# Attention and SwiGLU FFN on one core: the V loads on another DMA queue, and the q parts of the FFN's last products in other places

## The chip, the cores and the metric

The kernel runs on one core of a Trainium2 chip. A core has TensorE (matrix products, PE in the profile; PEld are its weight loads), VectorE (DVE), ScalarE (ACT) and GpSimd (POOL), and SyncE (SP), which computes nothing and issues DMAs. Each engine works off its own queue in program order, and the engines wait for each other by semaphores. A DMA is issued by an instruction in the queue of an engine (SPq and ACTq are the rows of SyncE and ScalarE that do this); the 16 DMA engines of the core then carry it out. The metric is the time of one execution on the device in microseconds, and of several runs the median.

## What is computed

The reference, cut to what matters (B=1, S=2048 rows, D=640; 32 heads of 192; the window W is the last 512 keys; F=1536):

```
xn = layernorm(x)
q = xn @ wq                                  # 32 heads of 192
p = softmax(q @ k[-512:].T * 192**-0.5)      # by head
s = concat(p @ v[-512:]) @ wo
g = silu((silu(xn @ w_gate) * (xn @ w_up)) @ w_down)
out = x + s * g
```

## The kernel before, in words

The order of the instructions in each engine's queue is that of the program text: a manual schedule, in which the framework only adds the waits.

*FFN part (to about 168 us of the profile).* The rows are worked on in four blocks of 512 (b = 0 to 3). For a block, `ffn_hidden` makes twelve groups of columns (f) of silu(gate) * up into the tile hT. The product with w_down is made by `ffn_down(b, u)`, two units a block (u = 0, 1), each with seven products of sums (Strassen's scheme in Winograd's form) in place of eight: w1, w2, w6, w5_, w7, w3, w4, six matmuls of 320 columns each (L456), called in this order, and then `rest`. Three PSUM banks U, V, W of a ring of four take the products; ScalarE copies banks out (L474, L484, L490) and makes the gates (`gate`, L465), VectorE adds (`total`, L462). S1 to S4 are sums of hT columns that are the left sides of w5_, w6, w7 and w3; S1 and S2 are made inside w1. The units of block b - 1 are spread among the column groups of block b; those of the last block have nothing to be spread among. At L678 to L687 they are run one after the other, and among their products the kernel puts six q parts, `q_full(i, j)` for the first two row blocks of head pair 0 (five matmuls of 512 columns into one bank of a score tile, L517, and a copy by ScalarE, L521), and the six sums that are left in the list `xwork` (VectorE, L537). After each product `do()` of number n = 0 to 6, a q part follows for n in (0, 3, 5), and one of `xwork` for each n from 1 on while there is one. The list is empty after the first unit. Behind `rest` of the second unit, ScalarE loads the table for Exp (L688).

*Attention part (to about 705 us).* Heads go in 16 pairs. A pair has four row blocks and two halves; a half is a scores phase (`scores_phase`) and a stretch of contexts (`stretch`). The scores phase has eight `scores` (6 products each into a score tile of PSUM, L777, then Exp by ScalarE into p_t, L781; two such tiles are in rotation), and in slots between them the products that make q of a later half: `differences` (L723), `sides` (L723, copied by ScalarE from PSUM to m_f, L753), `across` (VectorE and GpSimd), `third(0)`, `sums`, `third(1)` (the two `third` are `q_rows`: L709 and a sum by VectorE, L714). `third(0)` writes the PSUM tile that `sides` used, so it waits for the copy L753. The first half of a pair has one group more, `q_diag` (L723, copied by VectorE). The program order on ScalarE at the start of a half is: Exp of the first scores, copy of `sides`, and Exp of the second scores.

The stretch then makes four units of contexts, p times V (L816), in the order of `CONTEXTS`; V_p, one buffer for a head pair, is the right side. At the end of a unit `divide(i, q2)` divides by the row sums (VectorE L834 and L839, ScalarE L845) into O_b, and asks SyncE for a DMA that transposes O_b into OT_b (L848). The last unit of a pair is block 3 with q2 = 1.

`beside(pr, n)` puts side work behind scores n = 0 to 15 of pair pr. At n = 0 it asks for the transpose of the next pair's K on SyncE (`transpose_k`, L192), and then for V of this pair (`load_v(pr)`): two DMAs of 192 KB, one a head, on ScalarE's queue (L182). At n = 10 and 12 it loads wq and K of the pair after the next (SyncE, L148 and L137), and at n = 4, 5, 12, 13 `spill` stores finished OT_b blocks to DRAM (SyncE, L857).

*Last part (to the end).* The product with wo, again seven products for eight (L931), the gate and the store.

Of the kernel before, what the change touches and what calls it, by code (L numbers as in the profile page):

```python
# [10 lines left out]
ALU = mybir.AluOpType  # L11
# [4 lines left out]
def kernel(  # L16
# [13 lines left out]
    nc = tc.nc  # L30
# [14 lines left out]
    NB = Sq // 512  # L45
# [34 lines left out]
    def sc_tile():  # L80
        return sc_pool.tile([P, 2, 512], f32, name="sc")

    def mm_tile(which=None):
        which = mm_next[0] if which is None else which
        mm_next[0] = 1 - which
        return mm_pool[0].tile([P, 2, 512], f32, name="mm", tag="mm%d" % which)
# [92 lines left out]

    def load_v(pr):  # L180
        for h in range(2):
            nc.scalar.dma_start(  # L182
                out=V_p[:, :, h, 0:Dh],
                in_=vv[2 * pr + h, k0:Sk, :].rearrange("(p j) d -> p j d", j=KC),
            )

    def transpose_k(pr):
        d = pairs[pr]
        d["KT"] = kpool.tile([P, KC * 3, P], bf, name="KT")
        d["ssum"] = kpool.tile([P, 3], f32, name="ssum")  # L190
        d["nmean"] = kpool.tile([P, 3], f32, name="nmean")
        nc.sync.dma_start_transpose(  # L192
            out=d["KT"][:, :, :], in_=d["K"][:, :, :, :].rearrange("p j h d -> p (j h d)")
        )
# [4 lines left out]
    def sum_k(pr, c):  # L199
        nc.vector.reduce_sum(pairs[pr]["ssum"][:, c : c + 1], chunk_of_k(pr, c), axis=AX.XY)  # L200
# [3 lines left out]
    def centre_k(pr, n):  # L204

        d = pairs[pr]
        if n == 0:
            d["khat"] = kpool.tile([P, 3, W], bf, name="khat", bufs=2)
            nc.vector.tensor_scalar(d["nmean"][:], d["ssum"][:], -1.0 / W, None, op0=ALU.mult)
        t, dst, c, src = CENTRE[n]  # L210
        nc.vector.tensor_scalar(
            d["khat"][dst, t, :].rearrange("p (j n) -> p j n", n=P), chunk_of_k(pr, c)[src],
            d["nmean"][src, c : c + 1], None, op0=ALU.add,
        )
# [8 lines left out]
    def q_of(i, j):  # L223
        return q_pair(i)[:, 3 * (i % 2) + j, :]
# [4 lines left out]
    with ExitStack() as fctx:  # L229
# [190 lines left out]
        def carve(k, n):  # L420
            part, room[k] = room[k][:, 0:n], room[k][:, n:]
            return part
# [6 lines left out]
        S1, S2, S3, S4 = (carve(k, KD * P).rearrange("p (c q) -> p c q", q=P) for k in (1, 2, 2, 3))  # L429
# [12 lines left out]
        def ffn_down(b, u):  # L442

            if not down_banks:
                down_banks.extend(t[:, n, 0:HC] for t in (mm_tile(), mm_tile()) for n in range(2))
            at = 3 * (2 * b + u)
            U, V, W = (down_banks[(at + k) % 4] for k in range(3))
            g = {}

            def a(side, k):  # L450
                rows = slice((u + 2 * side) * P, (u + 2 * side + 1) * P)
                return hTs[b][:, k * KD : (k + 1) * KD, rows]

            def mm(m, left, ps, first=True):
                for c in range(KD):
                    nc.tensor.matmul(  # L456
                        ps, left[:, c, :], D_OF[m][:, c, :],
                        start=(first and c == 0), stop=(c == KD - 1), skip_group_check=True,
                    )

            def total(to, x, y, op=ALU.add):
                nc.vector.tensor_tensor(to, x, y, op)  # L462

            def gate(side, n, x):
                nc.scalar.activation(g[side][:, n * HC : (n + 1) * HC], x, ACT.Silu)  # L465

            def store(side):
                nc.sync.dma_start(out=g_d[4 * b + u + 2 * side, :, :], in_=g[side][:])

            def w1():  # L470
                for side in range(2):
                    g[side] = ffa.tile([P, D], bf, name="g_t", bufs=2)
                mm(W1, a(0, 0), U)
                nc.scalar.copy(p1, U)  # L474
                total(S1, a(1, 0), a(1, 1))
                total(S2, S1, a(0, 0), ALU.subtract)

            def w2():
                mm(W2, a(0, 1), V)
                total(p1, V, p1)  # L480

            def w6():
                mm(W6, S2, U, False)
                nc.scalar.copy(u2, U)  # L484
                gate(0, 0, p1)
                total(S3, a(0, 0), a(1, 0), ALU.subtract)

            def w5_():
                mm(W5, S1, W)
                nc.scalar.copy(w5, W)  # L490
                total(S4, a(0, 1), S2, ALU.subtract)

            def w7():
                mm(W7, S3, U, False)
                total(w5, U, w5)

            def w3():
                mm(W3, S4, W, False)
                total(u2, W, u2)
                gate(1, 1, w5)  # L500

            def w4():
                mm(W4, a(1, 1), U, False)
                gate(1, 0, U)
                store(1)

            def rest():
                gate(0, 1, u2)
                store(0)

            return [w1, w2, w6, w5_, w7, w3, w4], rest

        def q_full(i, j):
            pr, b = divmod(i, NB)
            q_ps = sc_tile()[:, 0, :]
            for c in range(NC):
                nc.tensor.matmul(  # L517
                    q_ps[:, :], pairs[pr]["wq"][:, AS_IS[j], c, :], xnT[:, c, b * 512 : (b + 1) * 512],
                    start=(c == 0), stop=(c == NC - 1),
                )  # L520
            nc.scalar.copy(q_of(i, j), q_ps[:, :])  # L521
# [81 lines left out]
        xwork = []  # L603
# [74 lines left out]
        early_q = [(i, j) for i in range(2) for j in range(3)]  # L678
        for u in range(2):
            downs, rest = ffn_down(NB - 1, u)  # L680
            for n, do in enumerate(downs):
                do()
                if n in (0, 3, 5):
                    q_full(*early_q.pop(0))
                if xwork and n:
                    xwork.pop(0)()
            rest()  # L687
        nc.scalar.activation(act_t[:], one_t[:], ACT.Exp)  # L688
# [10 lines left out]
    last = NPAIR - 1  # L699
# [130 lines left out]
    def divide(i, q2, acc, by_dve):  # L830
        O_b, OT_b = Obs[i], OTs[i]
        r = smpool.tile([P, 2, 2, 1], f32, name="r")
        a_v = acc[:, :, :].rearrange("p k (h c) -> p k h c", h=2)
        nc.vector.reciprocal(r[:], a_v[:, :, :, Dh : Dh + 1])  # L834
        for k in range(2):
            qt = 2 * q2 + k
            a_k = a_v[:, k, :, :]
            if k in by_dve:
                nc.vector.tensor_tensor(  # L839
                    O_b[:, qt, :, :], a_k[:, :, 0:Dh], r[:, k, :, :].to_broadcast([P, 2, Dh]),  # L840
                    ALU.mult,
                )
                continue
            for h in range(2):
                nc.scalar.activation(  # L845
                    O_b[:, qt, h, :], a_k[:, h, 0:Dh], ACT.Copy, scale=r[:, k, h, :]
                )
        nc.sync.dma_start_transpose(  # L848
            out=OT_b[:, 6 * q2 : 6 * q2 + 6, :],
            in_=O_b[:, 2 * q2 : 2 * q2 + 2, :, :].rearrange("p t h d -> p (t h d)"),  # L850
        )

    def spill(i, eng=nc.sync, qts=slice(0, 4)):

        pr, b = divmod(i, NB)
        at = o_d[4 * b + qts.start : 4 * b + qts.stop, :, 3 * pr : 3 * pr + 3, :]
        eng.dma_start(  # L857
            out=at.rearrange("t p c q -> p t c q"),
            in_=OTs[i][:, 3 * qts.start : 3 * qts.stop, :].rearrange("p (t c) q -> p t c q", c=3),
        )  # L860
# [106 lines left out]
    def total(to, x, y, op=ALU.add):  # L967
        V.tensor_tensor(to, x, y, op)
# [80 lines left out]
    def beside(pr, n):  # L1049

        b, kc = divmod(n, KC)
        if pr < last:
            if n == 0:
                transpose_k(pr + 1)
            elif b == 2 and kc < 3:
                sum_k(pr + 1, kc)
            elif n >= 11:
                centre_k(pr + 1, n - 11)
        if n == 0:
            load_v(pr)  # L1060
        elif pr + 2 < NPAIR and n in (10, 12):
            (load_k if n == 12 else load_wq)(pr + 2)
        half, n8 = divmod(n, 2 * KC)
        prev = pr * NB + 2 * half - 2
        if prev >= 0 and n8 in (4, 5):
            spill(prev + n8 - 4)
        if (pr, n) in AHEAD:
            what, *args = AHEAD[pr, n]
            what(*args)
# [52 lines left out]
    i = last * NB  # L1122
# [70 lines left out]
```

## Time and profile before

| | |
|---|---|
| median of 3 runs | 890.23 us |
| the three runs | 888.45, 890.23, 895.27 us |
| profiled execution, its own time | 893.5 us |
| its span, first to last instruction | 891.7 us |
| mean granted clock of TensorE | 0.998 |
| instructions | 22945 |
| ScalarE's Exp of the scores (L781) | 256, mean 1024 ns, 253.7 us |
| first and last issue of V on ScalarE's queue | 169.6 and 680.9 us |

A row of the timeline reads: start in us, duration in us, engine, line, operation, output tile <- input tiles, shapes, count; in brackets the idle time of the engine just before and what ended it. Neighbouring instructions of one kind are merged into one row, whose duration is that from the first's start to the last's end. Matmuls overlap in the pipeline, so such a row reaches some 0.15 us into the next. A row of the table of waits reads: who waited <- for whom: us in total, times, longest. A row of a table of stretches reads: from:to, length, and then the busy time of PE, PEld, DVE, ACT and POOL in it with the number of instructions, the granted TensorE clock, the share of the DMA engines and GB/s. The chain of waits is the sequence of work and waits, followed back from the end of the run, that set the end.

### The profile page before, as it was taken

The page shows a single profiled execution, that of the slowest core. Times are in us where ns is not written, and L with a number is a line of the kernel's source. Part 1 is how long each engine was busy: PE and PEld are TensorE (multiplying, and loading weights), DVE is VectorE, ACT ScalarE, POOL GpSimd, SP SyncE. Part 2 cuts the span into 40 slices and gives each one's busy share as a digit, 9 for nine tenths or more (in the row PEclk, how much of TensorE's full clock was granted, in tenths as well). Part 3 has the DMA queues.
Part 4 walks back from the last instruction along what each step waited for, and adds up shares of the span by engine and source line. Part 5 has one row for each costly group of instructions (what it writes and reads, how often), then busy time and mean ns, then how long its engine had stood idle before and what let it go on. Part 6 is the DMA issues. An engine that isn't in the chain of part 4 may idle for free.

```text
span 891.7 us, 22945 instructions
## 1 busy us (share of the span) xinstructions
PE 872.3 (98%) x9641; PEld 577.4 (65%) x9657; DVE 603.6 (68%) x1028; ACT 427.7 (48%) x649; POOL 114.0 (13%) x217
## 2 busy tenths in 40 slices
PE   8999999999998999999999999999999999999998
PEld 5455555576675666666666766766756777777775
DVE  5766876676775776767767866866866457555553
ACT  4265433656764765666666666666666400000000
POOL 0000000012212132132132132132120000000000
PEclk9999999999999999999999999999999999999999
DMA  9669873367988979968989777969789998655510
GB/s 295 163 212 279 210 223 97 65 135 155 220 198 172 198 171 202 181 152 194 180 169 199 161 146 176 192 154 207 158 192 264 244 330 311 207 178 177 177 67 16
DMA packets 273432, 165.52 MB, mean 186 GB/s; under 512 B 174384, under 2 KB 268208, under 8 KB 272816
## 3 DMA queue, kind: packets, MB, share of 16 engines
q1 hardware_dynamic: 254928, 149.79, 69.4%
q10 hardware_dynamic: 18400, 14.26, 5.9%
q8 instruction: 76, 1.25, 0.6%
q14 instruction: 28, 0.23, 0.1%
HBM read 89.95 MB, written 40.24 MB: 146 GB/s over the span
## 4 chain that ended last, share of the span: by engine, by line
PE 86%; DMA 6%; ACT 2%; ACTq 2%; DVE 2%; SPq 1%; issue 1%; DVEq 0%
PE acc L931 19%; PE sc L777 15%; PE sc L394 11%; PE mm L723 10%; PE mm L816 9%; PE sc L816 8%; PE mm L709 8%; PE mm L456 5%; DMA OT_b<-O_b 3%; ACTq L182 2%; ACT m_f L753 2%; DMA o_d<-OT_b 1%; PE sc L517 1%; DMA x_t<-in_A_x_dram 1%; DMA OT_b<-O_last 1%
## 5 line engine op out<-in xcount | busy, mean ns | idle before, releaser
L781 ACT ACTIVATE p_t<-sc 128x1024 bf16<-128x1024 f32 x256 | 253.7, 1024 | 61.9 <-PE sc L777 57.3
L777 PE MATMUL sc<-qT,khat 64*128 64x512 bf16 x1536 | 198.7, 377 | 0.0
L816 PEld LDWEIGHTS <-p_t 64*128 64x128 bf16 x4096 | 173.0, 94 | 8.6
L777 PEld LDWEIGHTS <-khat 64*128 64x128 bf16 x1536 | 89.2, 94 | 75.5 <-issue 1.0
L816 PE MATMUL mm<-V_p,p_t 64*128 64x193 bf16 x2112 | 111.6, 243 | 0.0
L816 PE MATMUL sc<-V_p,p_t 64*128 64x193 bf16 x1984 | 104.8, 243 | 0.0
L709 PE MATMUL mm<-xnT,wq_p 64*128 64x512 bf16 x660 | 84.0, 380 | 10.9 <-ACT m_f L753 9.9
L723 PE MATMUL mm<-xc,wq_p 64*128 64x512 f16 x750 | 94.5, 376 | 0.0
L931 PEld LDWEIGHTS <-a_s 128*128 128x128 f16 x768 | 75.1, 98 | 29.2
L714 DVE TENSOR_REDUCE qT<-mm 128x512 bf16<-128x1024 f32 x66 | 80.6, 1223 | 16.1 <-PE mm L709 13.7
L761 POOL TENSOR_TENSOR m_f<-m_f 128x1024 f32<-128x1024 f32 x28 | 65.7, 2348 | 189.2 <-DVE qT L756 189.2
L723 PEld LDWEIGHTS <-wq_p 64*128 64x128 f16 (+1 forms) x1050 | 58.5, 94 | 48.2 <-issue 0.6
L845 ACT ACTIVATE O_b<-sc,r 128x192 bf16<-128x192 f32 x120 | 43.9, 418 | 87.2 <-PE sc L816 87.2
L931 PE MATMUL acc<-b_w,a_q 128*128 128x320 bf16 (+1 forms) x576 | 81.8, 299 | 0.2 <-ACT xc L981 0.2
L931 PE MATMUL acc<-b_w,a_s 128*128 128x320 f16 (+1 forms) x576 | 81.8, 299 | 0.0
L981 ACT COPY xc<-acc 128x320 f32<-128x320 f32 x8 | 3.4, 428 | 141.6 <-PE acc L931 95.7
L931 PEld LDWEIGHTS <-a_q 128*128 128x128 bf16 x576 | 56.3, 98 | 22.4 <-issue 0.6
L709 PEld LDWEIGHTS <-wq_p 64*128 64x128 bf16 x660 | 36.8, 94 | 49.3 <-issue 18.7
L756 DVE TENSOR_TENSOR qT<-mm,m_f 128x1024 bf16<-128x1024 f32 x30 | 36.7, 1225 | 43.7 <-ACT m_f L753 43.7
L394 PE MATMUL sc<-xnT,wu_sb 128*128 128x512 bf16 (+1 forms) x260 | 60.3, 354 | 0.6 <-DMA wu_sb<-in_B_w_up_dram 0.6
L394 PE MATMUL sc<-xnT,wg_sb 128*128 128x512 bf16 (+1 forms) x247 | 59.7, 353 | 1.0
L401 ACT ACTIVATE sg<-sc 128x512 bf16<-128x512 f32 x46 | 27.3, 595 | 68.0 <-PE sc L394 66.2
(110 smaller groups left out, 907.9 us busy)
## 6 DMA issues: line engine op xcount, KB each, us to landing
o_d<-OT_b SPq DMA_DIRECT2D x64, 384.0 KB, 5.5
a_q<-o_d SPq DMA_DIRECT2D x28, 768.0 KB, 5.8
won<-in_A_wo_dram SPq DMA_DIRECT2D x24, 320.0 KB, 4.2
wo_d<-wo_s SPq DMA_DIRECT2D x24, 320.0 KB, 2.9
wq_rows<-in_A_wq_dram SPq DMA_DIRECT2D x16, 480.0 KB, 4.9
wq_rows<-in_A_wq_dram SPq DMA_DIRECT2D x30, 240.0 KB, 6.0
K_p<-in_A_k_cache_dram SPq DMA_DIRECT2D x32, 192.0 KB, 6.2
V_p<-in_A_v_cache_dram ACTq DMA_DIRECT2D x32, 192.0 KB, 4.0
```

Source lines behind the costliest of these rows:

```text
L394: nc.tensor.matmul(out, w_sb[:, c, f * P : (f + 1) * P], xnT[:, c, qc], start=(c == 0), stop=(c == NC - 1),)
L456: nc.tensor.matmul(ps, left[:, c, :], D_OF[m][:, c, :], start=(first and c == 0), stop=(c == KD - 1), skip_group_check=True,)
L709: nc.tensor.matmul(q_ps[:, h, :], w[r, AS_IS[j], c, :], xnT[r, c, b * 512 : (b + 1) * 512], start=(c == 0), stop=(c == NC - 1),)
L714: nc.vector.reduce_sum(q_of(i, j), q_ps[:, :, :].rearrange("p h n -> p n h"), axis=AX.X)
L723: nc.tensor.matmul(ps[:, h, :], ws[h][r, c, :], xs[h][r, c, :], start=(first and c == 0), stop=(c == NC - 1), skip_group_check=True,)
L756: nc.vector.tensor_tensor(q_pair(i)[:, 1:4:2, :], st["ps"][:, :, :], m_f[:, SIDE_S, ::-1, :], ALU.add)
L761: eng.tensor_tensor(m_f[:, SIDE_S, :, :], diag, m_f[:, SIDE_S, :, :], ALU.subtract)
L777: nc.tensor.matmul(sc[:, h, :], khat[r, j, ks], q_of(i, j)[r, :], start=(j == 0), stop=(j == 2))
L781: nc.scalar.activation(p_t[:, :, :], sc[:, :, :], ACT.Exp, scale=scale)
L816: m = nc.tensor.matmul(acc[:, k, h * 256 : h * 256 + Dh + 1], Ps[i][kc][r, h, qt * P : (qt + 1) * P], V_p[r, kc, h, 0 : Dh + 1], start=(p ...
L845: nc.scalar.activation(O_b[:, qt, h, :], a_k[:, h, 0:Dh], ACT.Copy, scale=r[:, k, h, :])
L931: nc.tensor.matmul(ps[k] if ns > 1 else ps, at[:, c, :], b_w[m][:, c, k * w : (k + 1) * w], start=(first and c == 0), stop=(c == KH - 1), ...
```

## The change

Two things, in one diff.

V: `load_v` issues on `nc.sync` in place of `nc.scalar`. V of pair 0 is still asked for behind the first scores of pair 0 (`beside`, n = 0, behind `transpose_k(1)`), now on SyncE. V of each later pair is asked for in `divide` of the last unit of the pair before, behind the division and ahead of the last transpose of that pair; SyncE then waits for the last contexts, which read the one buffer V_p.

FFN: in the two last units the q parts stand otherwise. In the first unit one is put ahead of w1, then one behind each of the products 3 (w5_) and 6 (w4); in the second, behind 1 (w2), 3 and 6. The sums of `xwork` follow products 1, 3 and 5 of each unit. S1 and S2 of the first of these units are asked for when the unit is set up, ahead of its products.

```
     def load_v(pr):
         for h in range(2):
-            nc.scalar.dma_start(
+            nc.sync.dma_start(
...
+            def sums():
+                total(S1, a(1, 0), a(1, 1))
+                total(S2, S1, a(0, 0), ALU.subtract)
+
             def w1():
...
                 mm(W1, a(0, 0), U)
                 nc.scalar.copy(p1, U)
-                total(S1, a(1, 0), a(1, 1))
-                total(S2, S1, a(0, 0), ALU.subtract)
+                if (b, u) != (NB - 1, 0):
+                    sums()
...
+            if (b, u) == (NB - 1, 0):
+                sums()
             return [w1, w2, w6, w5_, w7, w3, w4], rest
...
             downs, rest = ffn_down(NB - 1, u)
+            if u == 0:
+                q_full(*early_q.pop(0))
             for n, do in enumerate(downs):
                 do()
-                if n in (0, 3, 5):
+                if n in ((3, 6), (1, 3, 6))[u]:
                     q_full(*early_q.pop(0))
-                if xwork and n:
+                if xwork and n in (1, 3, 5):
                     xwork.pop(0)()
             rest()
...
+        pr, b = divmod(i, NB)
+        if (b, q2) == (NB - 1, 1) and pr < last:
+            load_v(pr + 1)
         nc.sync.dma_start_transpose(
             out=OT_b[:, 6 * q2 : 6 * q2 + 6, :],
...
-        if n == 0:
-            load_v(pr)
+        if n == 0 and pr == 0:
+            load_v(0)
         elif pr + 2 < NPAIR and n in (10, 12):
             (load_k if n == 12 else load_wq)(pr + 2)
```

## The prediction, made before the result was known

> **What bounds the kernel now.** I read the page first (busy times), then the waits, then for the place that the waits name the timeline, the chain and the stretches of two neighbouring stages, and at last the same views for the end of the FFN part. The page, the table of waits and the table of DMA issues:
>
> ```profile
> span 891.7 us, 22945 instructions
> PE 872.3 (98%) x9641; PEld 577.4 (65%) x9657; DVE 603.6 (68%) x1028; ACT 427.7 (48%) x649; POOL 114.0 (13%) x217
> PE mm L709 <- ACT m_f L753: 9.9, 14, 2.9
> V_p<-in_A_v_cache_dram ACTq DMA_DIRECT2D x32, 192.0 KB, 4.0
> K_p<-in_A_k_cache_dram SPq DMA_DIRECT2D x32, 192.0 KB, 6.2
> ```
>
> TensorE is busy 98% of the span, so only two things can move the time: TensorE's work, which the change leaves as it is, and its gaps, 891.7 - 872.3 = 19.4 us together. Half of them are one wait, met 14 times: the products of L709 (third part of q) wait until ScalarE has copied the "side" product out of PSUM (L753). An engine that is 48% busy makes the bound one wait, because of what stands in its queue. One stage with the wait (half 0 of a pair, from 306.80) and the next one without it (half 1, from 324.32), first ScalarE, then TensorE:
>
> ```profile
> 308.74 1.02 ACT L781 ACTIVATE p_t<-sc 128x1024 bf16<-128x1024 f32 x1
> 308.80 1.47 ACTq L182 DMA_DIRECT2D V_p<-in_A_v_cache_dram  x2
> 310.37 1.01 ACT L753 COPY m_f<-mm 128x1024 f32<-128x1024 f32 x1 [0.61 <-PE mm L723]
> ...
> 326.26 1.02 ACT L781 ACTIVATE p_t<-sc 128x1024 bf16<-128x1024 f32 x1
> 327.40 1.01 ACT L753 COPY m_f<-mm 128x1024 f32<-128x1024 f32 x1
> ```
> ```profile
> 306.80 1.26 PE L723 MATMUL mm<-xc,wq_p 64*128 64x512 f16 x10
> ...
> 311.44 1.26 PE L709 MATMUL mm<-xnT,wq_p 64*128 64x512 bf16 x10 [0.36 <-ACT m_f L753]
> 318.99 0.85 PE L816 MATMUL mm<-V_p,p_t 64*128 64x193 bf16 x16
> 324.32 1.26 PE L723 MATMUL mm<-xc,wq_p 64*128 64x512 f16 x10
> ...
> 328.46 1.26 PE L709 MATMUL mm<-xnT,wq_p 64*128 64x512 bf16 x10
> ```
>
> In both stages the first exp starts 1.94 us after the stage. In half 1 the copy follows 1.14 us later and L709 starts 4.14 us into the stage, with no gap. In half 0 the two V loads stand between exp and copy: 1.63 us instead of 1.14, and L709 starts at 4.64. Exp and V issue overlap only in part: the next engine instruction isn't dispatched before the queue is past the loads. The chain shows why 1.47 us for two loads:
>
> ```profile
> 308.80 0.55 ACTq L182
> ...
> 309.73 0.55 ACTq L182
> ```
>
> Two issues of 0.55 us and a pause of 0.38 between them. The price by stretches (span, then PE busy; PEclk and DMA share near the end):
>
> ```profile
> 202.20:677.43 475.23, 466.00 (x6473) 314.38 (x6470) 342.84 (x590) 305.54 (x420) 102.98 (x181) 1.00 0.85 183
> 269.06:290.82 21.76, 18.85 (x242) 12.06 (x238) 11.86 (x21) 10.97 (x15) 4.77 (x8) 0.92 0.79 157
> 276.00:279.00 3.00, 2.75 (x14) 1.24 (x15) 1.70 (x2) 2.04 (x3) 1.47 (x1) 0.56 1.23 290
> 306.80:324.32 17.52, 17.16 (x241) 11.49 (x238) 11.85 (x21) 10.97 (x15) 4.78 (x8) 1.00 0.79 166
> 324.32:340.30 15.98, 15.98 (x231) 10.99 (x228) 12.63 (x23) 10.86 (x15) 2.75 (x5) 1.00 0.96 214
> ```
>
> **V moved to SyncE's queue.** Removed: 32 issues on ScalarE's queue. Added: the same 32 on SyncE's; V of pair 0 behind pair 0's first scores, V of each later pair behind the last contexts of the pair before, ahead of that pair's last transpose. No TensorE, VectorE or GpSimd instruction is added or taken.
> What a half 0 needs without the wait is half 1 plus the one group that half 0 has more, q_diag, ten products:
>
> ```profile
> 291.00 1.08 PE mm L723 x10
> ```
>
> so 15.98 + 1.08 = 17.06 us, and the stage of 306.80 pays 17.52 - 17.06 = 0.46 for its V. From the first half 0 with such a load (202.20) to that of the last pair (677.43) lie 14 pairs: 475.23 - 14 x (15.98 + 17.06) = 475.23 - 462.56 = 12.7 us. The last pair comes on top:
>
> ```profile
> 682.54 1.25 PE L709 MATMUL mm<-xnT,wq_p 64*128 64x512 bf16 x10 [0.83 <-ACT m_f L753]
> ```
>
> From 677.43, where that stretch ends, 5.11 us to L709 instead of 4.14, so 1.0. Together 13.7 us, if each half 0 becomes like half 1. Of this, 21.76 - 17.06 = 4.7 us lie in one stage, 269.06, where the gap of up to 2.9 us was followed by 3 us at a granted clock of 0.56. The 13.7 exceed the 9.9 of the wait table, since the drain of TensorE's pipeline no longer hides behind the next product in a gap, and by this clock.
> [...]
> What is paid instead: SyncE's issues. Its queue in the same stage:
>
> ```profile
> 306.52 2.89 SPq L848 DMA_TRANSPOSE OT_b<-O_b  x2
> 309.51 1.46 SPq L848 DMA_TRANSPOSE OT_b<-O_b  x1
> 311.02 2.20 SPq L192 DMA_TRANSPOSE KT<-K_p  x1
> ```
>
> The load's own wait, for TensorE's last contexts (done by 306.80 plus the pipeline's drain), is over when SyncE is through with the third transpose at 306.52 + 2.89 = 309.41. Two issues of 0.55 and their pauses, some 1.2 us (between 1.1 and the 1.5 of ScalarE's queue), then push back the fourth transpose to about 310.7, KT to 312.2, and the spills behind them. Who waits for those: the fourth transpose frees an O_b that is written again a stage later, KT is summed in half 1 only. I cost this at nothing; without that cover it is 1.2 x 15 = 18 us. V itself is asked for at 309.5 and 310.0 instead of 308.8 and 309.7, and is needed at 318.99 - 0.46 = 318.5. Pair 0's V goes behind KT of pair 1 on SyncE, with its first contexts over ten microseconds later: nothing. ScalarE's next limit in half 0 is the same exp as in half 1, and VectorE's part comes earlier by what the copy does. From both sides: 13.7 us if all goes as in half 1; 15 x 0.46 = 6.9 us if only the plain issue time is won and the longer waits, which come from SyncE's own traffic, return in another form. I take 13.7, since half 1 shows ScalarE beside the same traffic and without one gap.
>
> **The FFN's last products.** Six q parts (five products each) and six VectorE sums (xc) stay, in other places. TensorE around the first and the last of them:
>
> ```profile
> 146.79 0.98 PE L456 MATMUL mm<-m_f,hT 128*128 128x320 f16 x6
> 148.30 0.97 PE L456 MATMUL mm<-wd_sb,hT 128*128 128x320 bf16 x6 [0.53 <-ACT g_t L465]
> 149.11 1.24 PE L517 MATMUL sc<-xnT,wq_p 128*128 128x512 bf16 x5
> 150.19 0.98 PE L456 MATMUL mm<-wd_sb,hT 128*128 128x320 bf16 x6
> 151.82 0.43 PE L456 MATMUL mm<-wq_p,khat 128*128 128x320 f16 x2 [0.65 <-DVE qT L462]
> ...
> 165.10 1.24 PE L517 MATMUL sc<-xnT,wq_p 128*128 128x512 bf16 x5
> 166.18 0.98 PE L456 MATMUL mm<-m_f,hT 128*128 128x320 f16 x6
> 167.68 1.25 PE L709 MATMUL mm<-xnT,wq_p 64*128 64x512 bf16 x10 [0.53 <-ACT g_t L465]
> ...
> 175.74 0.61 PE L709 MATMUL mm<-xnT,wq_p 64*128 64x512 bf16 x4 [0.33 <-DVE qT L714]
> ```
>
> First gap: w1 waits at 148.30 for a gate that reads its PSUM bank; a group of six follows the one before after 0.82 us, so it could have begun at 147.61. A q part of 1.08 us put there needs only a score bank that is long free, and w1 then starts at 148.69 behind the gate. Won: 0.69. The second gap (w6 behind w2, 0.65) stays: w2 and w6 are still neighbours. Last gap: the same at 167.68, 1.50 us behind w4 instead of 0.82; with the sixth q part in between, 0.68 is won. The other shifts (q parts behind w4 of the first unit and w2 of the second) put work between groups that had no gap; the three VectorE sums that go to the second unit, 0.7 to 1 us each, meet an idle VectorE. Moving S1 and S2 ahead changes no order on VectorE: 0.
> Against it: ScalarE now copies the sixth q part ahead of the last gate, the table load and the first exp:
>
> ```profile
> 166.38 0.59 ACT L521 CAST qT<-sc 128x512 bf16<-128x512 f32 x1 [0.83 <-PE sc L517]
> 167.53 0.46 ACT L465 ACTIVATE g_t<-qT 128x320 bf16<-128x320 f32 x1
> 169.62 1.02 ACT L781 ACTIVATE p_t<-sc 128x1024 bf16<-128x1024 f32 x1
> ```
>
> Counted from w4's start: copy from 0.82 + 1.28 = 2.1 to 2.7, gate, then exp 2.09 us behind the gate's start, so at 4.8 to 5.8. The third scores need its bank at 5.4: some 0.4 us of wait, and it hides in the wait of 0.33 at 175.74 (with the drain about 0.5), which a VectorE chain sets. Part two: 1.4 us, or 1.0 without that cover.
>
> **Sum.** 13.7 + 1.4 = 15.1 us. The profiled execution took 893.5 us (span 891.7 and 1.8 around it): 878.4. The median of the runs shown is 890.23, 3.3 below the profiled execution; the 4.7 us of one stage are the likeliest reason, so a usual execution wins 11 to 12 and ends at the same time. Were the 3.3 something else, it would be 890.23 - 15.1 = 875.1. I take **878**.
>
> **Rivals.**
> *V lands too late (slower).* On SyncE's queue V has the transposes ahead of it. For it: the same 192 KB take 6.2 us from issue to landing as K on SyncE and 4.0 as V on ScalarE. Against it: asked for at 310.0 and with 6.2 it is there at 316.2, and is needed at 318.5. It decides from a landing time of 8.5 us on; at 9.5 the gain is gone (15 x 1.0), at 10.1 the kernel takes 893.5 - 15.1 + 15 x 1.6 = 902 us. [...]
> *Only the plain issue is won (no change by measure).* If a usual execution has only the 0.46 of each pair, or the long waits return in another form, 6.9 + 1.4 = 8.3 us come off the median: 882. For it: the one stage of 4.7. Against it: the wait stood above 0.36 in the last pair too (0.83).
> *The bubbles of the FFN part only move.* The first exp comes late and nothing hides it: 878.4 + 1.4 = 880.
>
> **Chances and numbers.** A measurement of this kernel can tell about 1%, 8.9 us, from no change: faster means below 881.3. Full gain, with or without part two: 0.72, 874 to 881. Only the plain issue: 0.18, 881 to 887. V late: 0.10, from 890 up, 0.08 of it beyond 1%. The range leaves out the last case and the edge of the second: 874 to 886. Faster by over 1%: 0.72; within 1%: 0.18 + 0.02 = 0.20; slower by over 1%: 0.08.
>
> **What the profile afterwards would show.** Right: no V on ScalarE's queue; the wait of L709 for L753 gone from the table (now 9.9 us); half 0 stages of 17.06 us; TensorE's gaps near 5 us; w1 and the first L709 without a wait for a gate. Wrong: contexts (L816) waiting for V_p; a half 0 over 17.3 us; a granted clock below 1 behind a new gap; a wait of L777 for the first exp.

## The result, and the profile after

| | before | after |
|---|---|---|
| median | 889.95 us (4 runs, 888.45 to 895.27) | 879.3 us (4 runs, 878.91 to 880.1) |
| profiled execution | 893.5 us | 878.91 us |
| its span | 891.7 us | 877.1 us |

The ratio of the runs is 0.9871, 95% interval 0.983 to 0.9912; between the medians lie 10.7 us, 1.2%. The runs also lie closer together. The page of the changed kernel, then its table of DMA issues (line numbers have moved: V's issues are still L182, scores L785, contexts L824, differences and sides L731, third L717, the copy of sides L761, q parts L523):

```profile
span 877.1 us, 22922 instructions
PE 867.6 (99%) x9641; PEld 576.2 (66%) x9657; DVE 603.5 (69%) x1028; ACT 427.5 (49%) x649; POOL 114.2 (13%) x217
```
```profile
K_p<-in_A_k_cache_dram SPq DMA_DIRECT2D x32, 192.0 KB, 5.8
V_p<-in_A_v_cache_dram SPq DMA_DIRECT2D x32, 192.0 KB, 3.2
```

TensorE's gaps are 877.1 - 867.6 = 9.5 us instead of 19.4, and its busy time fell as well, from 872.3 to 867.6. Its table of waits no longer has a row of the third part for the copy of sides; what is left around the FFN's end is this:

```profile
PE mm L456 <- DVE qT L462: 0.7, 1, 0.7
PE mm L456 <- ACT qT L478: 0.6, 1, 0.6
...
PE mm L717 <- DVE qT L722: 0.4, 1, 0.4
```

The same stages as before, now from 300.29, and the stretch of the same 14 pairs:

```profile
201.28:663.91 462.63, 462.49 (x6473) 313.83 (x6470) 342.68 (x590) 305.55 (x420) 102.96 (x181) 1.00 0.87 188
300.29:317.31 17.02, 17.02 (x241) 11.50 (x238) 11.85 (x21) 10.97 (x15) 4.77 (x8) 1.00 0.89 171
317.31:333.29 15.98, 15.98 (x231) 10.99 (x228) 12.63 (x23) 10.86 (x15) 2.75 (x5) 1.00 0.94 215
```

Half 0 takes 17.02 us, TensorE busy in all of it. The 14 pairs take 462.63 us; the prediction had 462.56 for them. ScalarE and SyncE in that half 0:

```profile
302.23 1.02 ACT L789 ACTIVATE p_t<-sc 128x1024 bf16<-128x1024 f32 x1
303.37 1.01 ACT L761 COPY m_f<-mm 128x1024 f32<-128x1024 f32 x1
```
```profile
298.44 4.55 SPq L859 DMA_TRANSPOSE OT_b<-O_b  x3
303.08 1.25 SPq L182 DMA_DIRECT2D V_p<-in_A_v_cache_dram  x2
304.43 1.26 SPq L859 DMA_TRANSPOSE OT_b<-O_b  x1
305.75 1.35 SPq L192 DMA_TRANSPOSE KT<-K_p  x1
```

The copy follows the exp by 1.14 us, as in half 1, and the V issues stand on SyncE between the third and the fourth transpose, 2.8 us into the stage. TensorE at the end of the FFN part:

```profile
146.30 0.98 PE L456 MATMUL mm<-m_f,hT 128*128 128x320 f16 x6
147.11 1.24 PE L523 MATMUL sc<-xnT,wq_p 128*128 128x512 bf16 x5
148.19 0.98 PE L456 MATMUL mm<-wd_sb,hT 128*128 128x320 bf16 x6
149.74 0.98 PE L456 MATMUL mm<-wd_sb,hT 128*128 128x320 bf16 x6 [0.57 <-ACT qT L478]
151.37 0.97 PE L456 MATMUL mm<-wq_p,khat 128*128 128x320 f16 x6 [0.65 <-DVE qT L462]
...
174.82 1.26 PE L717 MATMUL mm<-xnT,wq_p 64*128 64x512 bf16 x10 [0.37 <-DVE qT L722]
```

Put together from the two traces, the span fell by 891.7 - 877.1 = 14.6 us. Up to the group at 146.30 (146.79 before) 0.49 us, in a part that the change doesn't touch; over the traces of all kernels here this group starts between 145.34 and 147.13, so the 0.49 isn't the change's. From there to the product at 174.82 (175.74 before) 28.52 us instead of 28.95: the FFN's last products brought 0.43. From there to the end 702.28 us instead of 715.96: V brought 13.68. That is for this pair of executions: the medians differ by 10.7 us, and the profiled execution of the kernel before was one of its longer ones.

### The profile page after: what moved, and what is told of

Its sections match the earlier page's. It is cut to its first block, busy times and chain, and to the rows that moved or that the text cites. A ratio compares the mean times of both kernels' runs of the same rounds, so it can differ in the third digit from the quotient of the medians.

```text
span 877.1 us, 22922 instructions
## 1 busy us (share of the span) xinstructions
PE 867.6 (99%) x9641; PEld 576.2 (66%) x9657; DVE 603.5 (69%) x1028; ACT 427.5 (49%) x649; POOL 114.2 (13%) x217
## 4 chain that ended last, share of the span: by engine, by line
PE 96%; DMA 1%; SPq 1%; DVE 1%; issue 0%; ACT 0%; ACTq 0%; DVEq 0%
PE acc L942 19%; PE sc L785 18%; PE mm L731 13%; PE sc L394 11%; PE mm L824 10%; PE sc L824 9%; PE mm L717 8%; PE mm L456 5%; PE sc L523 1%; DMA OT_b<-O_last 1%; DMA wg_sb<-in_B_w_gate_dram 1%; PE gu L394 0%; SPq L921 0%; DVE wq_p L174 0%; SPq L859 0%
## 5 line engine op out<-in xcount | busy, mean ns | idle before, releaser
L785 PE MATMUL sc<-qT,khat 64*128 64x512 bf16 x1536 | 198.1, 376 | 0.0
L824 PEld LDWEIGHTS <-p_t 64*128 64x128 bf16 x4096 | 173.0, 94 | 8.6
L785 PEld LDWEIGHTS <-khat 64*128 64x128 bf16 x1536 | 89.0, 94 | 75.2 <-issue 0.5
L824 PE MATMUL mm<-V_p,p_t 64*128 64x193 bf16 x2112 | 111.6, 243 | 0.0
L824 PE MATMUL sc<-V_p,p_t 64*128 64x193 bf16 x1984 | 104.8, 243 | 0.0
L731 PE MATMUL mm<-xc,wq_p 64*128 64x512 f16 x750 | 94.4, 376 | 0.0
L731 PEld LDWEIGHTS <-wq_p 64*128 64x128 f16 (+1 forms) x1050 | 58.4, 94 | 47.9
L717 PE MATMUL mm<-xnT,wq_p 64*128 64x512 bf16 x660 | 83.0, 376 | 0.5 <-DVE qT L722 0.4
L717 PEld LDWEIGHTS <-wq_p 64*128 64x128 bf16 x660 | 36.4, 94 | 36.8 <-issue 5.6
```

Of the source, the lines that this page charges most:

```text
L717: nc.tensor.matmul(q_ps[:, h, :], w[r, AS_IS[j], c, :], xnT[r, c, b * 512 : (b + 1) * 512], start=(c == 0), stop=(c == NC - 1),)
L731: nc.tensor.matmul(ps[:, h, :], ws[h][r, c, :], xs[h][r, c, :], start=(first and c == 0), stop=(c == NC - 1), skip_group_check=True,)
L785: nc.tensor.matmul(sc[:, h, :], khat[r, j, ks], q_of(i, j)[r, :], start=(j == 0), stop=(j == 2))
L824: m = nc.tensor.matmul(acc[:, k, h * 256 : h * 256 + Dh + 1], Ps[i][kc][r, h, qt * P : (qt + 1) * P], V_p[r, kc, h, 0 : Dh + 1], start=(p ...
```

## The experiments

### One part alone

V alone (both of its edits, FFN as before), and the FFN part alone (V as before):

```
-            nc.scalar.dma_start(
+            nc.sync.dma_start(
                 out=V_p[:, :, h, 0:Dh],
...
+        pr, b = divmod(i, NB)
+        if (b, q2) == (NB - 1, 1) and pr < last:
+            load_v(pr + 1)
...
-        if n == 0:
-            load_v(pr)
+        if n == 0 and pr == 0:
+            load_v(0)
```

V alone:

> V moved (queue and place), FFN part as before. My theory: V's two issues on ScalarE's queue held back the copy L753, and that is nearly all of the change: half 0 stages of 17.02 us as in the changed kernel, no wait of L709 for L753, some 13.7 us less: 876 to 880 us in the median, within 0.6 us of the changed kernel. Rival, the prediction's sum: the FFN part carries 1.4 us, so 880.7, 1.4 above the changed kernel.

Measured: 879.41 us (6 runs), ratio to the kernel before 0.9873 (0.9849 to 0.9897); the kernel before had 890.65 (18 runs). Half 0 takes 17.02 to 17.03 us in all pairs but three (17.12, 17.30 and 17.11). V alone is as fast as the whole change.

The FFN part alone:

> The FFN part alone, V on ScalarE's queue as before. My theory after reading the trace of the changed kernel: the wait of w1 for the gate (0.53) turns into a wait of w2 for the copy of p1 (0.57), because U and V are banks of one PSUM tile; only the last gap is won: 0.4 us, 889.5 us, no change that can be measured. Rival, the prediction's sum: 1.4 us, 888.6. L709's wait for L753 stays near 10 us in both.

Measured: 888.6 us (12 runs), ratio 0.9975 (0.9958 to 0.9993). By its trace the part between the same two points takes 28.53 us, so again 0.42 less than before, and w2 has the new wait (0.6 us); the third part's wait for the copy of sides was 6.4 us in this execution, 9.9 in that of before, and the stretch of the 14 pairs took 470.41 us instead of 475.23. The medians differ by 2.0 us, more than the trace of the FFN part gives; whether the shifted start of the attention part makes V's waits smaller or the executions merely vary (887.16 to 891.12) stays open. The prediction's 1.4 us lies inside the interval, but the trace shows that it didn't come about as worked out.

### Queue or place

Only the queue (SyncE, at the old place behind the first scores), and only the place (behind the last division, on ScalarE), each one half of the diff above.

Only the queue:

> V on SyncE's queue but asked for at the old place (behind the first scores of its own pair, so behind the fourth transpose and the transpose of K), FFN part as before. My theory: the queue alone does it; V is asked for some 2.7 us later than at the new place, at about 5.5 us of the stage, lands 3 to 6 us later and is needed at 11.7: no wait, same time as with V moved alone, 877 to 881. Rival: the place ahead of the last transpose is what brings the gain; then contexts wait for V and the time stays near 890.

Measured: 879.18 us (4 runs), ratio 0.9872 (0.9843 to 0.9901); half 0 is 17.02 to 17.03 us but for the same three pairs. V was asked for 5.6 us into the stage (306.07 in the stage from 300.45), behind KT, and nobody waited for it. On SyncE's queue the new place is worth nothing beyond the old one.

Only the place:

> V asked for at the new place (behind the last division of a pair) but still on ScalarE's queue, FFN part as before. My theory: the two issues (1.5 us) now stand ahead of the first exp and of the copy L753; the copy is as late as before or later, the gap of 0.46 us or more a pair stays, and the third scores may wait for the first exp as well: 888 to 896. Rival: the earlier place is what matters: near 880.

Measured: 884.9 us (5 runs), ratio 0.9929 (0.9902 to 0.9956). Neither: half the gain. My expectation counted both issues as ahead of the exp. ScalarE in this kernel:

```profile
302.06 0.42 ACT L845 ACTIVATE O_b<-sc,r 128x192 bf16<-128x192 f32 x1
302.10 0.56 ACTq L182 DMA_DIRECT2D V_p<-in_A_v_cache_dram  x1
302.37 0.42 ACT L845 ACTIVATE O_b<-sc,r 128x192 bf16<-128x192 f32 x1
302.76 0.59 ACTq L182 DMA_DIRECT2D V_p<-in_A_v_cache_dram  x1
303.40 1.02 ACT L781 ACTIVATE p_t<-sc 128x1024 bf16<-128x1024 f32 x1 [0.61 <-PE sc L777]
304.32 1.01 ACT L753 COPY m_f<-mm 128x1024 f32<-128x1024 f32 x1
```

The first issue runs beside the two last divisions, so only about one issue holds the exp back. The stage from 300.95 takes 17.31 us: 0.29 over the stage without any, where both issues behind the exp cost 0.46. And no pair has a wait of a microsecond or more: the longest half 0 is 17.74 us. Here an issue cost what of it no running instruction covered.

### More and fewer issues

V in four DMAs of 96 KB on ScalarE's queue, at the old place:

```
         for h in range(2):
-            nc.scalar.dma_start(
-                out=V_p[:, :, h, 0:Dh],
-                in_=vv[2 * pr + h, k0:Sk, :].rearrange("(p j) d -> p j d", j=KC),
-            )
+            for js in (slice(0, KC // 2), slice(KC // 2, KC)):
+                nc.scalar.dma_start(
+                    out=V_p[:, js, h, 0:Dh],
+                    in_=vv[2 * pr + h, k0:Sk, :].rearrange("(p j) d -> p j d", j=KC)[:, js, :],
+                )
```

> The kernel before, but V in four DMAs of 96 KB a pair on ScalarE's queue in place of two of 192 KB, same bytes and place. My theory: what costs is the time of the issues in ScalarE's queue ahead of L753; two more of 0.55 us and their pauses add 1.1 to 1.5 us a pair to the gap: 906 to 915 us. Rival: it is the bytes of V beside the other transfers, or a wait for a completion that comes anyway; then the time stays at 890.

Measured: 967.32 us (4 runs), ratio 1.0857 (1.0821 to 1.0893). The direction was right, the size was three to five times too small: 76.7 us instead of 15 to 24. The issues themselves are short (397 ns in the median); ScalarE waits between them. ScalarE's waits for this copy (L754 here), then the chain in one stage, then ScalarE's and TensorE's rows and the stretch of that stage:

```profile
ACT m_f L754 <- DMA OT_b<-O_b: 32.4, 8, 5.1
ACT m_f L754 <- DMA V_p<-in_A_v_cache_dram: 28.5, 7, 5.3
```
```profile
323.08 4.45 DMA OT_b<-O_b
327.53 0.02 issue
327.56 0.45 ACTq L183
```
```profile
322.48 0.37 ACTq L183 DMA_DIRECT2D V_p<-in_A_v_cache_dram  x1
322.53 1.02 ACT L782 ACTIVATE p_t<-sc 128x1024 bf16<-128x1024 f32 x1
322.89 5.11 ACTq L183 DMA_DIRECT2D V_p<-in_A_v_cache_dram  x3
328.10 1.01 ACT L754 COPY m_f<-mm 128x1024 f32<-128x1024 f32 x1 [4.55 <-DMA OT_b<-O_b]
```
```profile
329.16 2.32 PE L710 MATMUL mm<-xnT,wq_p 64*128 64x512 bf16 x10 [4.36 <-ACT m_f L754]
```
```profile
320.52:344.40 23.88, 19.52 (x241) 12.05 (x238) 11.86 (x21) 10.98 (x15) 4.77 (x8) 0.86 0.56 122
```

The last V issue goes off at 327.56, just when the fourth transpose, issued at 323.08, has landed: 0.03 us lie between the landing, 327.53, and the issue. V's data don't need that transpose; what ties the issue to it these views don't show. The longest of the waits that the table puts down to V_p, 5.3 us, ends likewise: with a V issue at 368.09, as the transpose issued at 363.37 has landed (368.07). In the trace of the kernel with only the place changed there is no such wait, and its longest half 0 is 17.74 us. So in the kernel before there was a second cost beside the issue time, and its chain shows it in the stages from 269.06 and from 340.30, where the second V issue starts as the first transpose lands:

```profile
267.21 7.30 DMA OT_b<-O_b
274.51 0.02 issue
274.53 0.55 ACTq L182
...
338.45 5.14 DMA OT_b<-O_b
343.62 0.04 issue
343.66 0.56 ACTq L182
```

The first of these is the stage that lost 4.7 us. Taken by pairs, half 0 of the kernel before is over 17.02 us by 14.1 us together (the changed kernel's by 0.5): 7.4 in the four pairs in which the second issue waited for a transpose (269.06, 340.30, 609.61 and the last), 3.2 in three pairs in which the second issue itself took 1.0 to 1.7 us, and 3.5 in the other eight, 0.27 to 0.50 each. With four issues the span grew by 75.0 us: TensorE's gaps by 46.0 and its busy time by 29.0, at a mean granted clock of 0.961. The gap of 4.36 us was again followed by a low clock: 0.60 from 326.00 to 332.00, and ten products took 2.32 us where 1.26 is usual.

If that is right, one V issue should be free even on ScalarE, at the old place, with all bytes:

```
-        for h in range(2):
-            nc.scalar.dma_start(
...
+        nc.scalar.dma_start(
+            out=V_p[:, :, :, 0:Dh],
+            in_=vv[2 * pr : 2 * pr + 2, k0:Sk, :].rearrange("h (p j) d -> p j h d", j=KC),
+        )
```

> The kernel before, but V of a pair in one DMA of 384 KB on ScalarE's queue in place of two of 192 KB; same bytes, queue and place. My theory: one issue of 0.55 us begins 0.06 us after the first exp does and ends under it (1.02 us), and it isn't the one that waits for a transpose of its own stage to land; the copy L753 is not held back, half 0 takes 17.02 us, and the time is that of V on SyncE's queue, 878.5 to 881. Rival: every issue on ScalarE's queue costs its time; then half the gain is left, 884 to 886. Second rival: the bytes of V at this place cost; then 890.

Measured: 879.22 us (4 runs), ratio 0.9885 (0.9863 to 0.9907); half 0 is 17.02 to 17.03 us in all pairs but two (17.13 and 17.11). ScalarE:

```profile
303.30 1.02 ACT L780 ACTIVATE p_t<-sc 128x1024 bf16<-128x1024 f32 x1
303.36 0.61 ACTq L181 DMA_DIRECT2D V_p<-in_A_v_cache_dram  x1
304.44 1.01 ACT L752 COPY m_f<-mm 128x1024 f32<-128x1024 f32 x1
```

The issue ends at 303.97, under the exp, and the copy follows the exp by 1.14 us as if there were no V at all. It was not the queue as such that cost, nor the bytes, but the part of the issues that no running instruction of ScalarE covers, and the waits between them.

The control, four issues on SyncE (the changed kernel with the split of the four DMAs):

> The changed kernel, but V in four DMAs of 96 KB a pair on SyncE's queue. My theory: issues on SyncE cost nothing there, four of them push the fourth transpose and K's back by another microsecond that nobody waits for: 878.5 to 881, where four on ScalarE's queue took 967. Rival: more issues cost on any queue, through the order of the transposes behind them: 885 or more.

Measured: 878.93 us (4 runs), ratio 0.9882 (0.9863 to 0.9901). On SyncE's queue four issues cost no more than two, and neither does what they push back.

### How late V may be

V of pairs 1 to 15 on SyncE behind scores n = 6 of its own pair:

```
-        if n == 0 and pr == 0:
-            load_v(0)
+        if n == (6 if pr else 0):
+            load_v(pr)
...
-        if (b, q2) == (NB - 1, 1) and pr < last:
-            load_v(pr + 1)
```

> The changed kernel, but V of pairs 1 to 15 is asked for on SyncE behind the scores n = 6 of its own pair, behind the spills: issued some 9 us into the stage, needed at 11.7. My theory: V lands 3.2 to 3.5 us after its issue also there, contexts wait 0.5 to 1.2 us a pair, 887 to 897 us in all. Rival, as the prediction had it for K's row: 6.2 us to landing, a wait of some 3.7 us a pair, with a low clock behind it: 930 or more.

Measured: 902.12 us (4 runs), ratio 1.0127 (1.0093 to 1.0161): the prediction's rival "V lands too late", brought about by an edit, and dearer than the 887 to 897 that I expected. Its profile, waits and then SyncE and TensorE in one stage (from 305.10):

```profile
PE mm L824 <- DMA V_p<-in_A_v_cache_dram: 18.0, 20, 3.0
```
```profile
312.60 2.63 SPq L182 DMA_DIRECT2D V_p<-in_A_v_cache_dram  x2
```
```profile
317.86 0.51 PE L824 MATMUL mm<-V_p,p_t 64*128 64x193 bf16 x8 [0.88 <-DMA V_p<-in_A_v_cache_dram]
```

V is issued 7.5 us into this stage, not some 9, but takes 4.2 us to landing in the median, not 3.2 to 3.5 as I expected and not the 6.2 of K's row. In this stage the first issue alone took 1.95 us, so the second went off at 314.61. The spills stand just ahead of both; whether their traffic slows V isn't shown. The contexts start 12.76 us into the stage instead of 11.69. So the rival's mechanism exists, and from 2.8 us (the new place) to 5.6 us (the old place on SyncE) there is room before it.

### The FFN's new wait

The trace after shows w2 waiting 0.57 us for ScalarE's copy of p1. The copy reads bank U, w2 writes bank V; in this unit both are halves of one PSUM tile. The same holds for w6 and the sum that reads V. A unit of the ring that starts at bank 3 has U in one tile, V and W in the other:

```
-            at = 3 * (2 * b + u)
+            at = 3 if (b, u) == (NB - 1, 0) else 3 * (2 * b + u)
```

In the changed kernel:

> The changed kernel, but the first of the two last units starts the ring of PSUM banks at 3, so that U lies in another tile than V and W. My theory: w2's wait for the copy of p1 (0.57) and w6's wait for VectorE's sum (0.65) come from the shared tile; both go, w1 to w6 follow each other without a gap, and the q part ahead of w1 covers the gate as the prediction had it: 1.4 us less than the changed kernel, 877.9. Rival: the waits are on the banks themselves or on S2; then they stay, 879.3.

Measured: 876.95 us (5 runs), ratio 0.9849 (0.9823 to 0.9875). Its TensorE:

```profile
145.75 0.98 PE L456 MATMUL mm<-m_f,hT 128*128 128x320 f16 x6
146.56 1.24 PE L523 MATMUL sc<-xnT,wq_p 128*128 128x512 bf16 x5
147.64 1.79 PE L456 MATMUL mm<-wd_sb,hT 128*128 128x320 bf16 x12
149.27 0.98 PE L456 MATMUL mm<-wq_p,khat 128*128 128x320 f16 x6
...
172.74 1.25 PE L717 MATMUL mm<-xnT,wq_p 64*128 64x512 bf16 x10 [0.38 <-DVE qT L722]
```

w1, w2 and w6 follow each other without a gap, and the part takes 26.99 us instead of 28.52: 1.53 less.

With V moved but the q parts in their old places:

> V moved as in the change, the same other start of the ring, q parts in the old places. My theory: w6's wait for VectorE's sum goes (0.65), w1's wait for the gate (0.53) and the first L709's (0.53) stay: 0.7 us less than V moved alone, 878.7, and about 0.8 to 1.3 more than with the q parts moved. Rival: the q parts carry nothing once the banks are apart; then this equals the kernel with the other ring and the q parts moved.

Measured: 878.49 us (6 runs), ratio 0.986 (0.9835 to 0.9885). The part takes 28.31 us (146.02 to 174.33) against 28.95 for V alone (145.87 to 174.82): 0.64 less, w6's wait. Between this kernel and the one with both lie 28.31 - 26.99 = 1.32 us: so much the new places of the q parts are worth once U and V lie in two tiles, and 0.43 when they don't. The kernel with the other start of the ring and the q parts moved has the lowest median of all, 2.3 us below the changed kernel's. The intervals of the two ratios overlap, so the times alone don't show that gain; the traces show 1.53 us of it in the FFN part.

## Why the prediction was right, point by point

- *The bound, and the term of V.* Right in place and size: 13.7 us from half 0 against half 1, 13.68 in the traces. What carried it was to take the stage without the wait as the measure of the stage with it; the table of waits alone said 9.9. In one thing it was wrong: it left TensorE's work as it is, took all of the gain out of the gaps and expected some 5 us of them afterwards. There are 9.5. The gaps fell by 9.9 us, the size of the wait, and the other 4.7 came out of TensorE's busy time; in the stage at 269.06, with its granted clock of 0.92, the same matmuls were busy for 18.85 us where they were for 17.16 at 306.80. For a usual execution the prediction said 11 to 12 us; the medians differ by 10.7, and V alone by 11.2.
- *Why V cost that.* Half right. The prediction had the issues and their pauses in ScalarE's queue. One of the two issues was covered by the exp; the second wasn't, and it also waited, in four pairs, for a transpose that it doesn't need. The prediction put the longer waits down to "SyncE's own traffic" and feared that they might return; four issues showed the wait, one issue its absence.
- *The covers on SyncE.* Right: the fourth transpose and KT came later and nobody waited, not even with four issues.
- *V lands too late.* Right as a mechanism, with the wrong measure for its size. K's 6.2 us were no measure for V on SyncE, which landed in 3.2 at the new place and in 3.5 at the old one. V took 4.0 on ScalarE and 3.5 on SyncE at the old place, 4.4 and 3.2 at the new one, so SyncE's queue didn't make it slower. That K stands behind three loads of wq may be the reason for its 6.2; no run here separates that.
- *First gap of the FFN, 0.69 won.* This step failed: "w1 then starts at 148.69 behind the gate. Won: 0.69." w1 did start 1.89 us behind the reference group (146.30; worked out were 1.90), but the q part that had stood between w1 and w2 had been the cover of w2's wait for the copy of p1. With it gone the wait came out, 0.57 and the drain of 0.16 (a group's row is 0.98 us long, the next group follows after 0.82 where nothing holds it), and w6 started 5.07 us behind that group, where it had been 5.03. The prediction looked at the pair w2 and w6 and not at the pair w1 and w2, which the edit made neighbours.
- *Last gap, 0.68 won, the late exp hidden.* 0.47 came (23.45 us from w6 to the last row instead of 23.92); a tenth each was lost ahead of the first L709 and in the scores that wait for the exp.
- *The sum.* 878.4 for the profiled execution, 878.91 measured; of 15.1 us 14.1 came (13.68 + 0.43), and 0.5 in the part ahead, which is luck: the FFN part brought 1.0 us less than forecast, and half of that was made up by a part that the change doesn't touch. That the median of before lay below its profiled execution by V's waits is likely but not shown, since only one execution of that kernel has a trace; after, where these waits are gone, median and profiled execution lie 0.4 us apart.

## What to carry to other kernels

Price a wait by the neighbouring stage of the same shape that doesn't have it, not by the table of waits. In this kernel a DMA issue in ScalarE's queue was free as long as an instruction of ScalarE ran over it (0.61 us under an exp of 1.02); count what sticks out, and look when the issue itself starts: with four issues the last one started as a transfer landed whose data it didn't need, 4.45 us after that transfer's own issue. When work is taken from between two instructions, ask of the pair that becomes neighbours whether they touch one tile.

## What had not been expected of the hardware

- A V DMA of 192 KB landed sooner from SyncE's queue than from ScalarE's: in 3.5 us against 4.0 at the old place and in 3.2 against 4.4 at the new one (medians).
- Gaps of 2.9 us and 4.4 us were followed by ten products in 2.24 and 2.32 us instead of 1.26, at a granted clock of 0.56 (kernel before, 276.00 to 279.00) and 0.60 (four issues on ScalarE, 326.00 to 332.00). The expectation for the four issues had counted no such loss.
- One half 0 took 17.30 us instead of 17.02 in the changed kernel, with V alone, with the queue alone and with four issues on SyncE, each time in the same pair, and 17.02 with the other start of the ring. In each of the four, ScalarE's copy of sides began 0.32 us late. The chain of the changed kernel calls that time "issue", which is time in which the engine waited for nothing that the profile shows:

```profile
468.55 0.02 ACTq L761
468.56 0.32 issue
468.88 1.02 ACT m_f L761
```

The same 0.32 us stands between the two V issues of the stage that the prediction priced (from 309.41 to 309.73 in the kernel before, where the chain calls it "issue" too). So that pause was neither V's issue nor a wait that the profile shows. What fills it no run here shows.
